# Weights' sign bits, the reciprocals' spread and a one-column minimum, from VectorE to GpSimd

## The chip, the core and the metric

The kernel runs on one core of a Trainium2 chip. The metric is the device time of one execution in microseconds (us). Engines are named as in the profile: PE (TensorE), DVE (VectorE), ACT (ScalarE), POOL (GpSimd) and SP (SyncE, which here only issues DMAs); PEld is PE's loading of weights.

## What is computed

Attention with a block-causal mask over 8 batches of 8 heads (576 tokens, head size 64), and on its output a two-layer feed-forward net with an unusual gate (`moe` in the names), 4608 tokens of width 512, hidden width 2048.

```
scores = scale * np.matmul(q, k.transpose(0, 1, 3, 2))
mask = block_i >= block_j
scores = np.where(mask, scores, -1000000000.0)
scores = scores - np.max(scores, axis=-1, keepdims=True)
attn = np.exp(scores)
attn = attn / (np.sum(attn, axis=-1, keepdims=True) + 1e-09)
attn_out = np.matmul(attn, v)
...
h = x @ w_in
sp = np.maximum(h, 0.0) + np.log1p(np.exp(-np.abs(h)))
g = h * erf(sp)
return (g @ w_out).astype(np.float32)
```

The weights come as 64-bit floats and are turned into numbers of the chip by the kernel itself.

## The kernel before

**Order.** Nothing runs in the order in which it is written. Every piece of work is recorded as a task by `Plan.add` (engine, assumed duration in ns, what it reads and writes, a priority), and `Plan.order` then plays the machine through with these assumed durations, always giving a free engine its ready task of the smallest priority. What comes out is one fixed instruction order for each engine; on the chip each engine works through its own list, and waits where an input or a buffer isn't there. Two things of this planner matter here. A DVE task that touches no PSUM is assumed to take longer while POOL is at work, by the share `SHARE` of what POOL's task still has to go. And the priority is a time in units of one head: head n has priority n, the decoding of the weights is spread from 0.5 and 6.5 on (`DEC0`, `DECR`), the net's units start at 12.5 (`MOE`) and follow each other by 0.93 (`STEP`).

**Weights** (`decode`, L326 to L331). Each of the 32 weight tiles arrives as 128 rows of 512 64-bit words (`raw`, four buffers in two tags). ACT scales the upper half of each word, read as a 32-bit float (L327). Two DVE instructions make a 32-bit word `sign` out of 16-bit quarters of the words: three low bits by a shift right by 13, and the sign bit by an and with 0x8000 (L329). A third DVE instruction shifts the scaled value left by 3 and ors `sign` in (L331). When all 16 tiles of a layer are there, their size is measured (L347 and what follows), and then each tile is split into two 16-bit parts, by ACT (L338) and DVE (L339).

**Heads** (64, in order). `split_qk` (L579, L580) splits keys and queries, and DMAs lay the parts out in one of three buffers `qk` (L583). `maxes` computes all scores `s` once on PE (L591); DVE takes the largest of every row, as six reductions (L595) of which the last two cover the halves of the fifth row block, and the minimum of these two (negated maxima, 64 rows by one column) is formed by L621. PE transposes the result (`mt`, L625), ACT copies it (L627) and a DMA puts it into `qk` as a further row, so that the second scores `t` (L643, L644) come with the maximum already taken off. ACT exponentiates (L648); the result is split in two parts `ph` and `pl`, of the first tile by ACT and DVE (L659, L661), of the second by POOL (L657, L661). PE multiplies with the values (`u`, L691) and sums (`us`, L720). `normalise` (four heads at a time) turns the sums by PE (`rt`, L738), takes reciprocals on DVE (L741), spreads them over columns into `rw` (L748, two instructions, DVE), transposes them on PE (`rb`, L755) and multiplies (L759, L762).

**The net** works in 72 units of 256 tokens by 512 hidden columns: PE `m_h` (L432), the gate on ACT and DVE (L392 to L414), PE `o` (L447).

**Filling.** 730 matmuls without a result (`warm`, L836) stand in PE's list between those of the first fourteen heads, by priority.

The values that `decode` takes with the shift and the and are whole 16-bit numbers; `words().bitcast(U16)` with t=4 names the quarters of a 64-bit word, quarter 3 holding the sign.

Of the kernel before, what the change touches and what calls it, by code (L numbers as in the profile page):

```python
# [13 lines left out]
U16 = mybir.dt.uint16  # L14
F32R = mybir.dt.float32r
AF = mybir.ActivationFunctionType
ALU = mybir.AluOpType
# [45 lines left out]
class Plan:  # L63
# [4 lines left out]
    SPARE = 300.0  # L68
    SWITCH = 90.0
    DRAIN = -0.7  # L70
    SHARE = 0.7
    HEAVY = 75.0
    ASIDE = 1.5

# [143 lines left out]
def tile_attention_moe(ctx: ExitStack, tc: tile.TileContext, qk, v, w, maskrows, sels, out):  # L218
    nc = tc.nc
    B, H, D2, S = qk.shape  # L220
    D = D2 // 2
    NT, DM = out.shape
    NF = w.shape[0]
    P = 128
# [18 lines left out]
    add = plan.add  # L243
# [71 lines left out]
    def decode(s, f):  # L315

        i = place(s, f)
        raw = buf("m", [P, UW], F32, ("r0", "r1")[f % 2], f"raw{s}_{f}", NR)
        words = lambda: raw()[:, : 2 * DM].bitcast(I32)
        top = lambda: words().rearrange("p (n t) -> p n t", t=2)[:, :, 1]  # L320
        val = lambda: home(i + 1)
        bits = lambda: val().bitcast(I32)
        bs = buf("m", [P, UW], F16, ("gh", "gl")[f % 2], f"sign{s}_{f}", NG)
        sign = lambda: bs().bitcast(I32)
        k, ks = ("W", i + 1), bs
        add("SP", 500, lambda: nc.sync.dma_start(words(), w[f, s].bitcast(I32)), w=[raw], lag=6000.0)  # L326
        add("ACT", 670, lambda: nc.scalar.activation(val(), f32(top()), AF.Copy, scale=2.0**-112), r=[raw], w=[k])  # L327
        for z, (op, val16) in enumerate(((ALU.logical_shift_right, 13), (ALU.bitwise_and, 0x8000))):
            add("DVE", 420, lambda z=z, op=op, val16=val16: nc.vector.tensor_scalar(out=sign().bitcast(U16).rearrange("p (n t) -> p n t", t=2)[:, :, z],  # L329
                in0=words().bitcast(U16).rearrange("p (n t) -> p n t", t=4)[:, :, 1 + 2 * z], scalar1=val16, scalar2=None, op0=op), r=[raw], w=[ks])  # L330
        add("DVE", 700, lambda: nc.vector.scalar_tensor_tensor(out=bits(), in0=bits(), scalar=3, in1=sign(), op0=ALU.logical_shift_left, op1=ALU.bitwise_or), r=[ks], w=[k])  # L331

    def split_weight(s, f):
# [251 lines left out]
    def maxes(n):  # L585
# [32 lines left out]
            red(4 + j, s, 0, 288, 64)  # L618

        def e():  # L620
            add("DVE", 300, lambda: nc.vector.tensor_tensor(out=mx[:64, 4:5], in0=mx[:64, 4:5], in1=mx[:64, 5:6], op=ALU.min), r=[("mx", n % 2, 5)], w=[("mx", n % 2, 4)])  # L621

        def f():
            pt = bank(f"mt{n}")
# [7 lines left out]
    def probs(n, out):  # L632

        K = D + 5
        sc = qsc[n // 4]
        klh, qhl, kh, qh = wide(n, 0), part(n, 1), wide(n, 2), part(n, 3)

        def one(j, q0, w_):
            kk = min(P, S - j * P)
            ks = slice(j * P, j * P + P)  # L640
            s = bank(f"t{j}_{n}_{q0}")

            add("PE", mmns(w_, True), lambda: nc.tensor.matmul(s()[:, :w_], lhsT=klh[:, ks], rhs=qhl[:, q0 : q0 + w_], start=True, stop=False), r=Q(n, "kl", "kc", "ql", "qc", "m"), w=[s])  # L643
            add("PE", mmns(w_, True), lambda: nc.tensor.matmul(s()[:, :w_], lhsT=kh[:K, ks], rhs=qh[:K, q0 : q0 + w_], start=False, stop=True), r=Q(n, "kh", "qh", "m"), w=[s])  # L644
            skip = max(0, starts[j] - q0)
            pt, c = offs[j]
            c += q0 + skip - starts[j]
            add("ACT", 190 + 0.84 * (w_ - skip), lambda: nc.scalar.activation(p32s[pt][n % NP[pt]][:kk, c : c + w_ - skip], s()[:kk, skip:w_], AF.Exp, scale=sc()[:kk, 1:2]),  # L648
                r=[s, sc], w=[("p32", pt, n % NP[pt], j, q0)])

        def split(pt, keys):
            p = p32s[pt][n % NP[pt]]
            ph = buf("a", [P, PN[pt]], F16, f"ph{pt}", f"ph{pt}_{n}", NPH)
            pl = buf("a", [P, PN[pt]], F16, f"pl{pt}", f"pl{pt}_{n}", NPH)
            keys = [("p32", pt, n % NP[pt], *k) for k in keys]
            if pt:
                add("POOL", 1100, lambda: nc.gpsimd.tensor_copy(ph(), p), r=keys, w=[ph])  # L657
            else:
                add("ACT", 850, lambda: nc.scalar.copy(ph(), p), r=keys, w=[ph])  # L659
            eng, ns, on = (("DVE", 1250, nc.vector), ("POOL", 2050, nc.gpsimd))[pt]  # L660
            add(eng, ns, lambda: on.tensor_tensor(out=pl(), in0=p, in1=ph(), op=ALU.subtract), r=keys + [ph], w=[pl])  # L661
            out.append((ph, pl))

        return [lambda: one(0, 0, 288), lambda: one(0, 288, 288), lambda: one(3, 320, 256),
                lambda: (one(4, 320, 256), split(0, [(0, 0), (0, 288), (3, 320), (4, 320)])), lambda: one(1, 128, 448),
                lambda: (one(2, 256, 320), split(1, [(1, 128), (2, 256)]))]

# [60 lines left out]
    def normalise(b, qd, usbs, rs, krs):  # L728
# [14 lines left out]
        def m(pp):  # L743
# [1 line left out]
            x16 = buf("a", [P, 2, S], F16, "x16", f"x16_{nm}_{pp}", 2)  # L745
            rw = buf("a", [P, 5, 2, D], F32, "rw", f"rw{nm}_{pp}", 1)
            for hf, k in enumerate((3, 2)):
                add("DVE", 430 - 100 * hf, lambda hf=hf, k=k: nc.vector.tensor_scalar(out=rw()[:, 3 * hf : 3 * hf + k], in0=ri()[:, pp, :k, hf, :].unsqueeze(3).broadcast_to([P, k, 2, D]),  # L748
                    scalar1=bsc[:, 8 * b + 2 + qd : 8 * b + 3 + qd], scalar2=None, op0=ALU.mult), r=[ri, ("bsc", b)], w=[(rw, hf)])
            for hf, (q0, q1) in enumerate(((0, 384), (384, 576))):  # L750
                rb = bank(f"rb{nm}_{pp}_{hf}")
# [194 lines left out]
```

## Time and profile before

| what | value |
|---|---|
| median of 3 runs | 1274.19 us (1273.89 to 1276.28) |
| the profiled execution, its own time | 1273.55 us |
| its span, first to last instruction | 1271.7 us |
| mean granted clock of PE | 0.974 |
| ACT busy | 935.4 us (74%) |
| DVE busy | 852.4 us (67%) |
| POOL busy | 177.2 us (14%), 154 instructions |
| read from and written to HBM | 55.61 MB and 18.87 MB |

The profile shows one execution. Its busy times are sums over instructions; a line of a group holds the source line, the engine, the operation, what is written and read, the shapes and the count, then busy us, the mean ns of one instruction, and the idle time of the engine just before them with what ended it. A line of the waits holds who waited for whom, the total in us, the number of times and the longest. A line of the timeline holds start and duration in us. PE's busy time is modelled: an instruction that is recorded as busy may stand in a pipeline.

### The profile page before, as it was taken

To read this page: it belongs to the slowest core of one execution; us is meant where nothing else is said; L and a number is where in the kernel's file an instruction comes from. 1 tells how busy PE (TensorE), PEld (TensorE's weight loads), DVE (VectorE), ACT (ScalarE), POOL (GpSimd) and SP (SyncE) were. 2 spreads that over 40 slices of the span, in tenths; PEclk is the share of its full clock that TensorE was granted. 3 is DMA by queue.
4 is the path that set the end of the run, shared out by engine and by line. 5 is a ranking of instruction groups with operands and counts; after the bars stand their busy time and mean duration, and the time that the engine had idled before them with its cause. 6 is when DMAs were issued, how large, how long until landed. Compare 5 with 4: busy or idle time off the path is not lost.

```text
span 1271.7 us, 25003 instructions
## 1 busy us (share of the span) xinstructions
PE 1199.7 (94%) x9984; PEld 834.3 (66%) x9984; DVE 852.4 (67%) x1689; ACT 935.4 (74%) x1517; POOL 177.2 (14%) x154
## 2 busy tenths in 40 slices
PE   5898899789999989999999999999999999999997
PEld 2577676456666667666676767666777677766664
DVE  5898799975757686867677676768677755433332
ACT  4687567777777777777677876877788877777774
POOL 0221212000111111112011111111101111000000
PEclk7899999889999999998999999999999999999999
DMA  7566551302313151323223231404122210010000
GB/s 242 164 196 203 159 150 45 99 15 72 98 41 101 41 143 41 85 67 100 75 76 87 67 101 41 126 16 136 48 84 62 74 56 20 27 49 28 18 18 17
DMA packets 80674, 104.52 MB, mean 82 GB/s; under 512 B 10399, under 2 KB 61599, under 8 KB 80558
## 3 DMA queue, kind: packets, MB, share of 16 engines
q1 hardware_dynamic: 69678, 93.39, 24.7%
q10 hardware_dynamic: 10880, 9.53, 3.2%
q8 instruction: 79, 1.29, 0.4%
q14 instruction: 37, 0.30, 0.1%
HBM read 55.61 MB, written 18.87 MB: 59 GB/s over the span
## 4 chain that ended last, share of the span: by engine, by line
PE 69%; ACT 6%; DVE 2%; issue 1%; DMA 1%; ACTq 1%; DVEq 0%
PE m_h L432 27%; PE o L447 26%; PE u L691 4%; ACT m_r L401 3%; PE s L591 3%; PE t L643 3%; PE t L644 2%; PE us L720 2%; ACT p L648 1%; PE rt L738 1%; PE rb L755 1%; DMA qk<-qhi 1%; DVE m_r L405 1%; ACTq L583 0%; DVE m_h L412 0%
## 5 line engine op out<-in xcount | busy, mean ns | idle before, releaser
L432 PE MATMUL m_h<-xh,wsb 128*128 128x256 f16 x2304 | 400.3, 274 | 4.3 <-ACT p L648 1.5
L432 PEld LDWEIGHTS <-wsb 128*128 128x128 f16 x3456 | 339.4, 98 | 57.8 <-issue 6.5
L401 ACT ACTIVATE m_r<-m_r,c 128x1024 f32<-128x1024 f32 x288 | 330.4, 1147 | 50.6 <-DVE m_r L405 32.4
L447 PE MATMUL o<-wsb,m_gh 128*128 128x512 f16 x1152 | 337.4, 384 | 12.2 <-ACT m_gh L413 12.2
L432 PE MATMUL m_h<-xl,wsb 128*128 128x256 f16 x1152 | 315.8, 274 | 0.0
L648 ACT ACTIVATE p<-t,qsc 128x288 f32<-128x288 f32 (+4 forms) x384 | 175.6, 479 | 107.8 <-PE t L644 104.0
L595 DVE TENSOR_REDUCE mx<-s 64x1 f32<-64x288 f32 (+4 forms) x384 | 166.3, 470 | 72.5 <-PE s L591 71.0
L447 PE MATMUL o<-wsb,m_gl 128*128 128x512 f16 x576 | 207.9, 382 | 0.0
L447 PEld LDWEIGHTS <-m_gh 128*128 128x128 f16 x1152 | 112.4, 98 | 128.5 <-ACT m_gh L413 15.2
L405 DVE SCALAR_TENSOR_TENSOR m_r<-m_r,m_r 128x1024 f32<-128x1024 f32 x72 | 90.3, 1254 | 157.3 <-ACT m_r L401 157.1
L657 POOL CAST ph<-p 128x768 f16<-128x768 f32 x64 | 63.5, 993 | 902.1 <-ACT p L648 838.3
L392 ACT ACTIVATE m_r<-m_h,c,bsc 128x512 f32<-128x512 f32 (+3 forms) x192 | 123.0, 671 | 36.1 <-PE m_h L432 35.7
L591 PE MATMUL s<-qk 68*128 68x256 f16 (+3 forms) x384 | 96.4, 314 | 28.9 <-DMA qk<-qhi 22.4
L643 PE MATMUL t<-qk 128*128 128x288 f16 (+3 forms) x384 | 114.5, 303 | 6.7 <-DVE mx L595 2.4
L412 DVE SCALAR_TENSOR_TENSOR m_h<-m_r,m_h 128x512 f32<-128x512 f32 x144 | 92.9, 689 | 40.8 <-ACT m_r L401 40.6
L644 PE MATMUL t<-qk 69*128 69x288 f16 (+3 forms) x384 | 114.5, 304 | 2.5 <-DMA qk<-mt 2.5
L836 PE MATMUL warm<-ident 128*128 128x256 f16 (+1 forms) x730 | 111.8, 289 | 1.5 <-POOL ident masks.py:199 1.5
L661 POOL TENSOR_TENSOR pl<-p,ph 128x768 f16<-128x768 f32 x64 | 111.2, 1737 | 5.1
L413 ACT CAST m_gh<-m_h 128x512 f16<-128x512 f32 x144 | 82.0, 585 | 31.9 <-DVE m_h L412 29.9
L414 DVE TENSOR_TENSOR m_gl<-m_h,m_gh 128x512 f16<-128x512 f32 x144 | 93.0, 682 | 10.6 <-ACT m_gh L413 9.4
L447 PEld LDWEIGHTS <-m_gl 128*128 128x128 f16 x576 | 56.6, 99 | 62.0 <-issue 1.3
L836 PEld LDWEIGHTS <-ident 128*128 128x128 f16 x730 | 71.8, 99 | 23.5 <-issue 2.5
(103 smaller groups left out, 1363.8 us busy)
## 6 DMA issues: line engine op xcount, KB each, us to landing
st<-qk SPq DMA_DIRECT2D x64, 288.0 KB
raw<-w SPq DMA_DIRECT2D x32, 512.0 KB
v<-v SPq DMA_DIRECT2D x16, 640.0 KB
qk<-qhi SPq DMA_DIRECT2D x128, 72.0 KB
qk<-qhi ACTq DMA_DIRECT2D x128, 72.0 KB
qk<-qlo SPq DMA_DIRECT2D x128, 72.0 KB
x_d<-x SPq DMA_DIRECT2D x32, 288.0 KB
out<-ob SPq DMA_DIRECT2D x36, 256.0 KB
```

Source lines behind the costliest of these rows:

```text
L392: add("ACT", 310 + 0.84 * w * (y - x) / T, lambda i=i, h=h, b=b, x=x, y=y, w=w: nc.scalar.activation(cut(br[0]()[:, i * w : (i + 1) * w], ...
L401: add("ACT", 300 + 0.834 * UW, lambda r=r, a=a, pp=pp: nc.scalar.activation(r(), a(), AF.Square, bias=const(pp[1]), scale=pp[0]), r=[a] + ...
L405: add("DVE", 160 + 1.05 * UW, lambda r=r, a=a, c=c, pp=pp, ops=ops: nc.vector.scalar_tensor_tensor(out=r(), in0=a(), scalar=pp[0], in1=c() ...
L432: nc.tensor.matmul(hk(k), lhsT=wf16(0, f, lo)[:, cc * P : (cc + 1) * P], rhs=x()[:, cc, :], start=cc == 0 and i == 0, stop=cc == NCC - 1 a ...
L447: nc.tensor.matmul(o[c](), lhsT=a()[:, sl], rhs=wf16(1, f, wlo), start=u == 0 and k == 0 and not lo and wlo == 0, stop=u == NU - 1 and k = ...
L591: add("PE", mmns(w_, True), lambda: nc.tensor.matmul(s()[:, c0 : c0 + w_], lhsT=qh[:K, i * P : i * P + P], rhs=kh[:K, k0 : k0 + w_], start ...
L595: add("DVE", 145 + 1.07 * w_, lambda: nc.vector.tensor_reduce(out=mx[:r, col : col + 1], in_=s()[:r, c0 : c0 + w_], axis=AX.X, op=ALU.max, ...
L643: add("PE", mmns(w_, True), lambda: nc.tensor.matmul(s()[:, :w_], lhsT=klh[:, ks], rhs=qhl[:, q0 : q0 + w_], start=True, stop=False), r=Q( ...
L644: add("PE", mmns(w_, True), lambda: nc.tensor.matmul(s()[:, :w_], lhsT=kh[:K, ks], rhs=qh[:K, q0 : q0 + w_], start=False, stop=True), r=Q( ...
L648: add("ACT", 190 + 0.84 * (w_ - skip), lambda: nc.scalar.activation(p32s[pt][n % NP[pt]][:kk, c : c + w_ - skip], s()[:kk, skip:w_], AF.Ex ...
L661: add(eng, ns, lambda: on.tensor_tensor(out=pl(), in0=p, in1=ph(), op=ALU.subtract), r=keys + [ph], w=[pl])
L836: t = add("PE", 220 if n is None else 150, lambda: nc.tensor.matmul(b_w()[:, : w * P], lhsT=ident16, rhs=ident16[:, None, :].broadcast_to( ...
```

## The change

`sign` is now made by two POOL instructions with arithmetic in place of bit operations: the low bits as value times 2^-13, at most 7; the sign bit as (value at least 32768) times 32768. The minimum L621 becomes a POOL instruction that takes the second column as a per-row scalar, and the spread L748 becomes a POOL instruction of the same form as before. The assumed durations of the tasks on POOL are new, as are two of the split's, and `SHARE` falls from 0.7 to 0.2.

```diff
-    SHARE = 0.7
+    SHARE = 0.2
...
-        for z, (op, val16) in enumerate(((ALU.logical_shift_right, 13), (ALU.bitwise_and, 0x8000))):
-            add("DVE", 420, lambda z=z, op=op, val16=val16: nc.vector.tensor_scalar(out=sign().bitcast(U16).rearrange("p (n t) -> p n t", t=2)[:, :, z],
-                in0=words().bitcast(U16).rearrange("p (n t) -> p n t", t=4)[:, :, 1 + 2 * z], scalar1=val16, scalar2=None, op0=op), r=[raw], w=[ks])
+        for z, (a, oa, b, ob) in enumerate(((2.0**-13, ALU.mult, 7.0, ALU.min), (32768.0, ALU.is_ge, 32768.0, ALU.mult))):
+            add("POOL", 700, lambda z=z, a=a, oa=oa, b=b, ob=ob: nc.gpsimd.tensor_scalar(out=sign().bitcast(U16).rearrange("p (n t) -> p n t", t=2)[:, :, z],
+                in0=words().bitcast(U16).rearrange("p (n t) -> p n t", t=4)[:, :, 1 + 2 * z], scalar1=a, scalar2=b, op0=oa, op1=ob), r=[raw], w=[ks])
...
-            add("DVE", 300, lambda: nc.vector.tensor_tensor(out=mx[:64, 4:5], in0=mx[:64, 4:5], in1=mx[:64, 5:6], op=ALU.min), r=[("mx", n % 2, 5)], w=[("mx", n % 2, 4)])
+            add("POOL", 150, lambda: nc.gpsimd.tensor_scalar(out=mx[:64, 4:5], in0=mx[:64, 4:5], scalar1=mx[:64, 5:6], scalar2=None, op0=ALU.min), r=[("mx", n % 2, 5)], w=[("mx", n % 2, 4)])
...
-                add("POOL", 1100, lambda: nc.gpsimd.tensor_copy(ph(), p), r=keys, w=[ph])
+                add("POOL", 1000, lambda: nc.gpsimd.tensor_copy(ph(), p), r=keys, w=[ph])
...
-            eng, ns, on = (("DVE", 1250, nc.vector), ("POOL", 2050, nc.gpsimd))[pt]
+            eng, ns, on = (("DVE", 1050, nc.vector), ("POOL", 1750, nc.gpsimd))[pt]
...
-                add("DVE", 430 - 100 * hf, lambda hf=hf, k=k: nc.vector.tensor_scalar(out=rw()[:, 3 * hf : 3 * hf + k], in0=ri()[:, pp, :k, hf, :].unsqueeze(3).broadcast_to([P, k, 2, D]),
+                add("POOL", 650 - 150 * hf, lambda hf=hf, k=k: nc.gpsimd.tensor_scalar(out=rw()[:, 3 * hf : 3 * hf + k], in0=ri()[:, pp, :k, hf, :].unsqueeze(3).broadcast_to([P, k, 2, D]),
                     scalar1=bsc[:, 8 * b + 2 + qd : 8 * b + 3 + qd], scalar2=None, op0=ALU.mult), r=[ri, ("bsc", b)], w=[(rw, hf)])
```

Since the planner's numbers change, it orders all engines anew. PE's list has the same instructions in another order.

DVE's list at its start before, from the scale of the first four heads to the first reductions (`sign_0` and `sign_1` are the words of the first two weight tiles, `qlo` a head's low part, `vm` and `vs` the values' scale):

```order
L329 TENSOR_SCALAR sign_0_225<-raw_0_167 128x512
L487 TENSOR_REDUCE vm_0_228<-v_0_0_163 128x1
L572 COPY qsc_235<-qb_230 128x2
L329 TENSOR_SCALAR sign_0_225<-raw_0_167 128x512
L331 SCALAR_TENSOR_TENSOR wsb<-wsb,sign_0_225 128x512
L492 TENSOR_REDUCE vs_0_247<-vt_0_240 1x1
L580 SCALAR_TENSOR_TENSOR qlo_252<-st_136,qsc_235,qhi_238 128x576
L580 SCALAR_TENSOR_TENSOR qlo_257<-st_142,qsc_235,qhi_249 128x576
L493 TENSOR_SCALAR vs_0_247<-vs_0_247 1x1
L494 RECIPROCAL vs_0_247<-vs_0_247 1x1
L329 TENSOR_SCALAR sign_1_263<-raw_1_172 128x512 x2
L331 SCALAR_TENSOR_TENSOR wsb<-wsb,sign_1_263 128x512
```

The same place of DVE's list in the changed kernel:

```order
L487 TENSOR_REDUCE vm_0_227<-v_0_0_163 128x1
L572 COPY qsc_240<-qb_231 128x2
L331 SCALAR_TENSOR_TENSOR wsb<-wsb,sign_0_223 128x512
L492 TENSOR_REDUCE vs_0_252<-vt_0_244 1x1
L493 TENSOR_SCALAR vs_0_252<-vs_0_252 1x1
L494 RECIPROCAL vs_0_252<-vs_0_252 1x1
L331 SCALAR_TENSOR_TENSOR wsb<-wsb,sign_1_235 128x512
L580 SCALAR_TENSOR_TENSOR qlo_270<-st_136,qsc_240,qhi_246 128x576
L503 COPY vsb_0_274<-vb_0_263 128x2
L580 SCALAR_TENSOR_TENSOR qlo_277<-st_142,qsc_240,qhi_259 128x576
L331 SCALAR_TENSOR_TENSOR wsb<-wsb,sign_2_248 128x512
```

The `sign` instructions are gone from DVE, three of the L331 stand ahead of the first reductions instead of two, and each of them now waits for POOL.

POOL's list before holds nothing but pairs of L657 and L661, two heads of which stand here (heads 2 and 3, `p_1_0` and `p_1_1` being the two buffers of the second probability tile):

```order
L657 CAST ph_2_778<-p_1_0_120 128x768
L661 TENSOR_TENSOR pl_2_794<-p_1_0_120,ph_2_778 128x768
L657 CAST ph_3_934<-p_1_1_121 128x768
L661 TENSOR_TENSOR pl_3_945<-p_1_1_121,ph_3_934 128x768
L657 CAST ph_4_1160<-p_1_0_120 128x768
```

POOL's list in the changed kernel around the same two heads, while the first layer's weights are decoded:

```order
L329 TENSOR_SCALAR sign_12_727<-raw_12_566 128x512 x2
L329 TENSOR_SCALAR sign_13_750<-raw_13_590 128x512 x2
L621 TENSOR_SCALAR mx_130<-mx_130 64x1
L329 TENSOR_SCALAR sign_14_841<-raw_14_759 128x512
L657 CAST ph_2_851<-p_1_0_120 128x768
L661 TENSOR_TENSOR pl_2_862<-p_1_0_120,ph_2_851 128x768
L329 TENSOR_SCALAR sign_14_841<-raw_14_759 128x512
L329 TENSOR_SCALAR sign_15_901<-raw_15_774 128x512 x2
L621 TENSOR_SCALAR mx_131<-mx_131 64x1
L657 CAST ph_3_966<-p_1_1_121 128x768
L661 TENSOR_TENSOR pl_3_980<-p_1_1_121,ph_3_966 128x768
L329 TENSOR_SCALAR sign_0_1155<-raw_0_1026 128x512 x2
```

The weights' `sign` words, each of which waits for the landing of its `raw`, now stand in one line with the heads' minima and with `ph`, which waits for ACT; all 16 tiles of the first layer stand ahead of head 3's `ph`, where DVE's list before had the L331 of ten tiles (`sign_0` to `sign_9`) ahead of head 3's L661.

## The prediction

> **What bounds the kernel now.** First the head of the page, with its 40 slices, each 31.8 us long.
>
> ```profile
> span 1271.7 us, 25003 instructions
> PE 1199.7 (94%) x9984; PEld 834.3 (66%) x9984; DVE 852.4 (67%) x1689; ACT 935.4 (74%) x1517; POOL 177.2 (14%) x154
> PE   5898899789999989999999999999999999999997
> DVE  5898799975757686867677676768677755433332
> PEclk7899999889999999998999999999999999999999
> ```
>
> PE is busy 94% of the span. From the tenth slice on it is at 9 nearly throughout, while DVE has fallen to 5 to 8; in slices two to eight DVE stands at 7 to 9, and there PE has holes. So there are two stages, and only the early one has DVE near its limit. The windows make this exact; their columns are busy us and count of PE, PEld, DVE, ACT and POOL, then granted clock, DMA share and GB/s.
>
> ```profile
> 0.00:13.00 13.00, 10.45 (x41) 4.28 (x41) 1.02 (x7) 5.91 (x14) 2.47 (x26) 1.00 0.76 268
> 13.00:190.00 177.00, 149.82 (x1446) 115.16 (x1447) 149.33 (x335) 117.30 (x239) 35.04 (x25) 0.92 0.60 180
> 190.00:284.00 94.00, 78.18 (x619) 53.05 (x617) 79.11 (x156) 69.93 (x111) 12.92 (x10) 0.89 0.20 55
> 284.00:1256.00 972.00, 952.94 (x7851) 658.68 (x7852) 619.10 (x1190) 738.17 (x1151) 126.73 (x94) 0.99 0.23 65
> 1256.00:1272.00 16.00, 8.33 (x30) 3.09 (x28) 3.81 (x5) 4.06 (x6) 0.00 (x0) 0.86 0.09 33
> ```
>
> From 13 to 190 us the weights are decoded, from 190 to 284 they are split while the net begins, and then heads and net run side by side. PE's list holds the same instructions after the change, so the time can fall only by PE's idle time and by what the clock takes. Idle are 27.2 us in the first window (177 - 149.8), 15.8 in the second, 19.1 in the 972 us of the third, 7.4 at the end. The clock takes 0.11 of 94 us, 10.3 us, in the second. In the first it takes 0.08 of 177, 14 us, but nearly all of that lies at the start, where PE runs filler. **What can be won lies before 284 us: 43.0 us of idle time and some 10 of clock.** Whose wait is it? The waits between 13 and 284 us:
>
> ```profile
> ACT p L648 <- PE t L644: 30.3, 29, 5.0
> PE s L591 <- DMA qk<-qhi: 18.8, 10, 6.0
> ACT wsb L338 <- DVE wsb L339: 14.2, 13, 3.4
> DVE mx L595 <- PE s L591: 13.9, 19, 2.8
> PE mt L625 <- DVE mx L621: 3.8, 1, 3.8
> PE o L447 <- ACT m_gh L413: 3.7, 1, 3.7
> ```
>
> 18.8 of the 43.0 us end with a DMA that brings a head's keys and queries, and 3.8 with the first head's minimum, in the startup. The rest, 20.4 us, is made of small waits on DVE and ACT. ACT waits 14.2 us for DVE's split, so behind the net's first units DVE is what comes last.
>
> **What is removed from DVE.** Groups of DVE up to 284 us:
>
> ```profile
> L329 DVE TENSOR_SCALAR sign<-raw 128x512 uint16<-128x512 uint16 x64 | 29.6, 501 | 0.0
> L339 DVE SCALAR_TENSOR_TENSOR wsb<-wsb,wrow 128x512 f16<-128x512 f32 x31 | 25.6, 825 | 2.1 <-ACT wsb L338 1.9
> L331 DVE SCALAR_TENSOR_TENSOR wsb<-wsb,sign 128x512 int32<-128x512 int32 x32 | 24.1, 753 | 0.9
> L661 DVE TENSOR_TENSOR pl<-p,ph 128x832 f16<-128x832 f32 x17 | 19.9, 1173 | 3.3 <-ACT ph L659 3.3
> L580 DVE SCALAR_TENSOR_TENSOR qlo<-st,qsc,qhi 128x576 f16<-128x576 f32 x20 | 17.6, 879 | 4.1 <-ACT qhi L579 4.1
> L621 DVE TENSOR_TENSOR mx<-mx 64x1 f32<-64x1 f32 x19 | 6.1, 322 | 0.1
> L748 DVE TENSOR_SCALAR rw<-ri,bsc 128x384 f32<-128x384 f32 x7 | 4.2, 597 | 0.0
> ```
>
> L329 gives 29.6 us, L621 6.1, and L748 4.2 with seven of its shorter form, 7 x 0.375 = 2.6 by its mean below. That is **42.5 us of DVE's 228.4 busy us between 13 and 284** (149.3 + 79.1), 19%. The three groups over the whole span stand below: after 284 us go 12 us of L621 and 25 x (0.602 + 0.375) = 24 us of L748 from a DVE that is busy 64% there; PE's 19.1 us of idle time in 972 is all that they could touch, and I count them as nothing. They are hidden behind PE's own list.
>
> ```profile
> L748 DVE TENSOR_SCALAR rw<-ri,bsc 128x384 f32<-128x384 f32 x32 | 19.3, 602 | 0.3
> L621 DVE TENSOR_TENSOR mx<-mx 64x1 f32<-64x1 f32 x64 | 18.0, 282 | 0.5
> L748 DVE TENSOR_SCALAR rw<-ri,bsc 128x256 f32<-128x256 f32 x32 | 12.0, 375 | 0.0
> ```
>
> **What POOL takes on.** Its groups up to 284 us:
>
> ```profile
> L661 POOL TENSOR_TENSOR pl<-p,ph 128x768 f16<-128x768 f32 x17 | 30.8, 1813 | 1.4
> L657 POOL CAST ph<-p 128x768 f16<-128x768 f32 x17 | 17.1, 1008 | 212.5 <-ACT p L648 193.4 <-PE s L591 11.1 <-PE t L643 7.9
> L472 POOL MEMSET rs<- 64x192 f32 x3 | 0.6, 253 | 0.0
> ```
>
> The trace shows no POOL instruction like the new ones. The nearest row is the cast: one input, one output. Over 512 in place of 768 columns it gives 1008 x 512/768 = 672 ns. From below the memset's 253 ns, with no input and fewer columns, bounds it; from above the two-input row, 1813 ns undivided. I take 0.67 us: 64 x 0.67 = 43 us for `sign`. L748 comes to 0.50 and 0.34 us in the same way, 6 us up to 284; L621, a single column, lies between nothing and the memset, 0.2 us or so, some 4 us for 19. POOL thus goes from 48 to about 101 us of 271: far from full. By the bounds `sign` would be 16 to 116 us, and POOL 74 to 174 of 271.
>
> The Trainium skill, page GPSIMD Engine Reference, section 3.1 (Elementwise), speaks against such a move: it keeps elementwise work on DVE, and gives 769 ns for a tight loop over 512 elements. By that figure, an estimate, `sign` would be 49 us; no run here shows it, and the sum would hardly differ.
>
> **What DVE loses again.** The two engines hold each other up. Rows of the timeline:
>
> ```profile
> 65.26 0.68 DVE L331 SCALAR_TENSOR_TENSOR wsb<-wsb,sign 128x512 int32<-128x512 int32 x1
> 72.14 1.13 POOL L657 CAST ph<-p 128x768 f16<-128x768 f32 x1 [7.29 <-ACT p L648]
> 72.48 0.79 DVE L621 TENSOR_TENSOR mx<-mx 64x1 f32<-64x1 f32 x1
> 83.99 0.97 POOL L657 CAST ph<-p 128x768 f16<-128x768 f32 x1 [8.87 <-ACT p L648]
> 84.31 1.19 DVE L331 SCALAR_TENSOR_TENSOR wsb<-wsb,sign 128x512 int32<-128x512 int32 x1
> ```
>
> An L331 with POOL idle takes 0.68 us. One that begins at 84.31, inside a cast that ends at 84.96, ends at 85.50: it stood still until POOL was done. The one-column minimum at 72.48 ended with the cast, at 73.27. Over the whole run the medians tell what such instructions take undisturbed (min/median/max):
>
> ```profile
> L331 DVE SCALAR_TENSOR_TENSOR wsb<-wsb,sign x32: 672/691/1312, 15.4 to 189.5; 128x512 int32<-128x512 int32 x32
> L339 DVE SCALAR_TENSOR_TENSOR wsb<-wsb,wrow x32: 719/747/2130, 181.7 to 284.1; 128x512 f16<-128x512 f32 x32
> L661 DVE TENSOR_TENSOR pl<-p,ph x64: 992/1012/2378, 39.5 to 1075.7; 128x832 f16<-128x832 f32 x64
> L580 DVE SCALAR_TENSOR_TENSOR qlo<-st,qsc,qhi x64: 797/810/2190, 18.1 to 1023.1; 128x576 f16<-128x576 f32 x64
> ```
>
> Against the means above, the loss up to 284 us is 32 x 62 ns = 2.0 us for L331, 31 x 78 = 2.4 for L339, 17 x 161 = 2.7 for L661 and 20 x 69 = 1.4 for L580: 8.5 us for 48 us of POOL, 0.18 per us. The 53 us that POOL takes on cost 9.5 at this rate. On top, an L331 comes when POOL has just finished its `sign` and may begin the next one: half an instruction each, 32 x 0.34 = 11 us at most; I take a third, 3.5. So DVE loses 13 and is **relieved by 42.5 - 13 = 29.5 us net**.
>
> **What becomes of it.** At most 20.4 us of idle time and 10.3 of clock, 31 in all, are within reach; the 18.8 us on the DMA are not, since keys and queries go through three buffers and their transfer as before. I take half of the idle time, 10, and a third of the clock, 3.5: the relief is 13% of DVE's early work, but the filler in PE's list is fixed in number and takes its time with DVE faster too. Against it stand new waits. The minimum now stands in POOL's list behind `sign` words that wait for their landing and behind `ph`, which waits for ACT; behind it wait `mt` on PE, and all that follows there. The cover is wide in the later stage:
>
> ```profile
> 342.43 0.14 DVE L621 TENSOR_TENSOR mx<-mx 64x1 f32<-64x1 f32 x1
> 346.04 0.27 PE L625 MATMUL mt<-ident,mx 128*5 128x128 f32 x1
> ```
>
> There PE takes the result 3.5 us after it is there, more than a cast and a two-input instruction of POOL (1.01 + 1.81 = 2.82 us). Without cover one head costs what the startup's wait cost, 3.8 us; I take one such, 4. The sum: 1273.55 - 10 - 3.5 + 4 = 1264.05, say **1264.5 us**, against the profiled execution's own 1273.55 (span 1271.7 and 1.85 around it); that execution lies 0.64 under the median of 1274.19.
>
> **Rivals.** *All of the relief arrives* (0.12): the new order closes the small waits and the clock stays up in the second window; 20.4 + 10.3 less 4 is 27, hence 1247. For it speaks that ACT waits for DVE there; against it that other engines are 74 to 83% busy too.
>
> *It was hidden anyway* (0.22): PE's early time is its filler, its DMA waits and the first units' chain through ACT (3.7 us on `m_gh`), and the relief only lets DVE wait longer, as it does already for 13.9 us on `s`. Then 1273.5, give or take 2.5. The other form of this is that the new instructions do not spare DVE anything, since the time that L621 spends waiting for POOL (mean 322 ns, 0.14 us in the row at 342.43) is spent on POOL's list instead.
>
> *POOL gives back more than it takes* (0.18), the one on the slow side. Place: L331 between 13 and 190 us. If a `sign` instruction takes as long as the two-input row, 1.81 us, POOL works 126 us more, which cost 0.18 x 126 = 23 us, and every L331 meets half an instruction, 32 x 0.9 = 29: 52 us lost against 42.5 won, DVE up by 9.5, time 1283. It decides from about 1.5 us per instruction on (0.18 x 106 + 32 x 0.75 = 43). Between the two the time lies between 1273.5 and 1283. The Trainium skill, page SBUF — State Buffer, section Who interferes with whom, tells of a pair of ports that VectorE and GpSimd share; whichever comes first holds it for its whole instruction, against a DVE instruction with two SBUF inputs too. By that rule every new POOL instruction can stop an L331; the row at 84.31 agrees.
>
> **How the numbers follow.** My forecast (1259 to 1270) has 0.48, the rivals 0.12, 0.22 and 0.18. A measurement of this kernel can tell some 0.2%, 2.5 us, from no change. Faster: 0.48 + 0.12 and a little of the second, 0.62. Same: 0.20. Slower: 0.18. For 8 in 10 the range leaves out the far half of the first rival and the far part of the last: 1250 to 1278.
>
> **What would show it.** Right: L329 on POOL near 0.67 us; DVE's busy time up to the last L339 down by about 30 us, and that L339 before 276 us in place of 284; L331's mean rising to 0.8 or 0.9 us; PE's idle time before the same place down by about 10; the later stage as it is. Wrong: `sign` at 1.5 us or more; L331 above 1.5; PE waiting for L621 on POOL in many heads; PE's waits for the DMA of `qhi` growing as the rest shrinks; or idle time coming up after 284 us, where all orders were made anew and I have assumed that PE does not mind.

## The result, and the profile after

The change makes the kernel slower: 1336.92 us (median of 4 runs, 1331.49 to 1338.15) against 1275.15 us (median of 4) for the kernel before on the same chip, a ratio of 1.0476 with a 95% interval of 1.0445 to 1.0508. The prediction said 1264.5. One execution of a later kernel, minimum and spread alone, took 1552.58 us at a granted clock of 0.751 and is left out of its median and ratio. The head of the page of the changed kernel:

```profile
span 1334.8 us, 25085 instructions
PE 1224.1 (92%) x9984; PEld 842.8 (63%) x9984; DVE 794.2 (59%) x1497; ACT 934.1 (70%) x1517; POOL 438.1 (33%) x346
PE   4587668998999999999999899999999999999997
DVE  3454447588675667676756666667676654443332
POOL 6998995121222222222213332323132323010000
PEclk7688769898999999999999999999999999999999
```

A slice is 33.4 us long. In the first six DVE has fallen from 5 to 9 to 3 to 5, as was wanted, but PE has fallen with it and POOL stands at 6 to 9. From slice eleven on PE is at 9 nearly throughout, as before. To measure this, take a point that both kernels pass: the fifth unit of the net, whose first matmul stands in the timelines (start, us, what) at 275.66 us before and at 336.31 after:

```profile
275.66 0.27 PE L432 MATMUL m_h<-xh,wsb 128*128 128x256 f16 x1
```

```profile
336.31 0.28 PE L432 MATMUL m_h<-xh,wsb 128*128 128x256 f16 x1
```

Three windows, the first 205 us, then up to that point and from there on, with the columns that the prediction gives; before:

```profile
0.00:205.00 205.00, 173.73 (x1600) 130.41 (x1601) 163.69 (x368) 134.93 (x270) 42.22 (x54) 0.93 0.58 177
...
13.00:276.00 263.00, 222.27 (x2015) 163.54 (x2016) 224.88 (x484) 180.01 (x341) 47.96 (x34) 0.91 0.48 141
276.00:1272.00 996.00, 967.00 (x7931) 666.45 (x7928) 626.48 (x1200) 749.45 (x1164) 126.73 (x94) 0.99 0.23 64
```

and after:

```profile
0.00:205.00 205.00, 136.15 (x983) 90.64 (x984) 93.40 (x190) 98.73 (x202) 180.33 (x120) 0.76 0.49 149
...
13.00:336.00 323.00, 241.73 (x1975) 170.60 (x1977) 189.81 (x373) 177.89 (x337) 215.53 (x126) 0.82 0.39 113
336.00:1335.00 999.00, 970.98 (x7974) 667.63 (x7968) 604.20 (x1123) 750.42 (x1168) 220.12 (x194) 0.99 0.23 65
```

The last rows are 996 and 999 us long, so **the loss lies before the net's fifth unit**: 60 us of it, for much the same number of matmuls (2015 and 1975). PE's idle time there grew from 40.7 us (263 - 222.27) to 81.3 (323 - 241.73), and its busy time by 19.5, with a clock of 0.82 in place of 0.91. In the first 205 us PE gets through 983 matmuls where it did 1600, while POOL is busy for 180 of the 205 us. What keeps POOL busy stands in its groups up to 345 us:

```profile
L329 POOL TENSOR_SCALAR sign<-raw 128x512 uint16<-128x512 uint16 x64 | 148.9, 2328 | 15.5 <-DMA raw<-w 11.5
L661 POOL TENSOR_TENSOR pl<-p,ph 128x768 f16<-128x768 f32 x16 | 28.2, 1764 | 1.4
...
L657 POOL CAST ph<-p 128x768 f16<-128x768 f32 x16 | 13.1, 821 | 8.4 <-ACT p L648 8.2
L621 POOL TENSOR_SCALAR mx<-mx 64x1 f32<-64x1 f32 x18 | 10.3, 574 | 69.6 <-DVE mx L595 44.6 <-DVE wone L359 14.3 <-DVE wmx L349 10.2
```

A `sign` instruction takes 2.33 us, not the 0.67 of the prediction; 64 of them are 149 us. With the 35 us that the heads' pairs took between 13 and 190 us before, that is 184 us, for a decoding whose last L331 started at 189.5 us then. It can't end before POOL is through; here the last `sign` instruction starts at 205.1 us and the last L331 at 224.1. The spread's groups on POOL, and DVE's four two-input groups up to 345 us:

```profile
L748 POOL TENSOR_SCALAR rw<-ri,bsc 128x384 f32<-128x384 f32 x6 | 9.0, 1498 | 9.3 <-DVE ri L741 9.0 <-PE warm L836 0.4
L748 POOL TENSOR_SCALAR rw<-ri,bsc 128x256 f32<-128x256 f32 x6 | 7.2, 1198 | 0.0
```

```profile
L339 DVE SCALAR_TENSOR_TENSOR wsb<-wsb,wrow 128x512 f16<-128x512 f32 x31 | 25.2, 812 | 4.8 <-ACT wsb L338 4.5
L331 DVE SCALAR_TENSOR_TENSOR wsb<-wsb,sign 128x512 int32<-128x512 int32 x32 | 25.1, 800 | 39.0 <-POOL sign L329 38.4 <-ACT wsb L327 0.6
L661 DVE TENSOR_TENSOR pl<-p,ph 128x832 f16<-128x832 f32 x17 | 19.4, 1138 | 11.4 <-ACT ph L659 11.4
L580 DVE SCALAR_TENSOR_TENSOR qlo<-st,qsc,qhi 128x576 f16<-128x576 f32 x20 | 17.7, 890 | 5.1 <-ACT qhi L579 5.0
```

L331 has risen only from 753 to 800 ns; what it costs is the 38.4 us of DVE's waiting for `sign`. The waits between 13 and 205 us show where PE stands (who waited for whom, us, times, longest):

```profile
PE mt L625 <- POOL mx L621: 41.9, 7, 11.0
DVE wsb L331 <- POOL sign L329: 38.4, 14, 6.0
...
DVE mx L595 <- PE s L591: 25.1, 10, 7.6
```

PE waits 41.9 us in seven pieces for the one-column minimum. One of them in the timeline (start, us, what, idle time before it):

```profile
153.58 10.63 POOL L329 TENSOR_SCALAR sign<-raw 128x512 uint16<-128x512 uint16 x5
...
164.16 0.29 POOL L621 TENSOR_SCALAR mx<-mx 64x1 f32<-64x1 f32 x1
164.24 1.76 DVE L331 SCALAR_TENSOR_TENSOR wsb<-wsb,sign 128x512 int32<-128x512 int32 x2 [5.26 <-POOL sign L329]
...
164.50 0.37 PE L625 MATMUL mt<-ident,mx 128*5 128x128 f32 x1 [6.79 <-POOL mx L621]
```

A minimum of 0.29 us stands behind five `sign` instructions, and PE stands with it for 6.79 us. So far the trace allows three causes: the minimum's place in POOL's list, the order of all lists, which was laid out for instructions of 0.7 us, and POOL's capacity, that is, more work than it can do in the time. The experiments take them apart.

### The profile page after: what moved, and what is told of

Its sections match the earlier page's. It is cut to its first block, busy times and chain, and to the rows that moved or that the text cites. A ratio compares the mean times of both kernels' runs of the same rounds, so it can differ in the third digit from the quotient of the medians.

```text
span 1334.8 us, 25085 instructions
## 1 busy us (share of the span) xinstructions
PE 1224.1 (92%) x9984; PEld 842.8 (63%) x9984; DVE 794.2 (59%) x1497; ACT 934.1 (70%) x1517; POOL 438.1 (33%) x346
## 4 chain that ended last, share of the span: by engine, by line
PE 67%; POOL 14%; ACT 7%; DVE 5%; issue 3%; DMA 2%; ACTq 1%; SPq 0%; POOLq 0%
PE m_h L432 26%; PE o L447 24%; POOL sign L329 9%; PE u L691 4%; POOL rw L748 3%; PE s L591 3%; ACT m_r L401 3%; PE t L643 2%; PE t L644 2%; DMA qk<-qhi 2%; PE us L720 2%; ACT p L648 1%; DVE mx L595 1%; PE rt L738 1%; POOL pl L661 1%
## 5 line engine op out<-in xcount | busy, mean ns | idle before, releaser
L621 POOL TENSOR_SCALAR mx<-mx 64x1 f32<-64x1 f32 x64 | 43.5, 680 | 409.0 <-DVE mx L595 362.5
L329 POOL TENSOR_SCALAR sign<-raw 128x512 uint16<-128x512 uint16 x64 | 148.9, 2328 | 15.5 <-DMA raw<-w 11.5
L836 PE MATMUL warm<-ident 128*128 128x256 f16 (+1 forms) x730 | 131.9, 315 | 1.5 <-POOL ident masks.py:199 1.5
L748 POOL TENSOR_SCALAR rw<-ri,bsc 128x384 f32<-128x384 f32 x64 | 77.0, 1209 | 144.6 <-DVE ri L741 130.8
L591 PE MATMUL s<-qk 68*128 68x256 f16 (+3 forms) x384 | 100.2, 323 | 20.7 <-DMA qk<-qhi 12.0
L661 POOL TENSOR_TENSOR pl<-p,ph 128x768 f16<-128x768 f32 x64 | 111.6, 1743 | 5.5
L657 POOL CAST ph<-p 128x768 f16<-128x768 f32 x64 | 56.8, 887 | 159.6 <-ACT p L648 159.1
```

Of the source, the lines that this page charges most:

```text
L329: add("POOL", 700, lambda z=z, a=a, oa=oa, b=b, ob=ob: nc.gpsimd.tensor_scalar(out=sign().bitcast(U16).rearrange("p (n t) -> p n t", t=2)[ ...
L591: add("PE", mmns(w_, True), lambda: nc.tensor.matmul(s()[:, c0 : c0 + w_], lhsT=qh[:K, i * P : i * P + P], rhs=kh[:K, k0 : k0 + w_], start ...
L836: t = add("PE", 220 if n is None else 150, lambda: nc.tensor.matmul(b_w()[:, : w * P], lhsT=ident16, rhs=ident16[:, None, :].broadcast_to( ...
```

## The experiments

The ratios are to the kernel before on the same chip, with 95% intervals. "Told" is the duration that `Plan.add` is given, from which the orders of all engines come.

**One part alone, with the change's numbers.** Three kernels: `sign` alone on POOL, the minimum and the spread alone, and the numbers alone with all three parts on DVE. The edits against the changed kernel; for the first:

```diff
-            add("POOL", 150, lambda: nc.gpsimd.tensor_scalar(out=mx[:64, 4:5], in0=mx[:64, 4:5], scalar1=mx[:64, 5:6], scalar2=None, op0=ALU.min), r=[("mx", n % 2, 5)], w=[("mx", n % 2, 4)])
+            add("DVE", 300, lambda: nc.vector.tensor_tensor(out=mx[:64, 4:5], in0=mx[:64, 4:5], in1=mx[:64, 5:6], op=ALU.min), r=[("mx", n % 2, 5)], w=[("mx", n % 2, 4)])
...
-                add("POOL", 650 - 150 * hf, lambda hf=hf, k=k: nc.gpsimd.tensor_scalar(out=rw()[:, 3 * hf : 3 * hf + k], in0=ri()[:, pp, :k, hf, :].unsqueeze(3).broadcast_to([P, k, 2, D]),
+                add("DVE", 430 - 100 * hf, lambda hf=hf, k=k: nc.vector.tensor_scalar(out=rw()[:, 3 * hf : 3 * hf + k], in0=ri()[:, pp, :k, hf, :].unsqueeze(3).broadcast_to([P, k, 2, D]),
```

> Only the sign words are made on POOL; the minimum and the spread are back on DVE; the planner's numbers are those of the change. Theory A (POOL's time: a sign instruction takes 2.1 to 2.3 us instead of 0.7, 64 of them fill POOL between 13 and 205 us, and whatever else stands in its list, minima above all, comes late): the minima no longer stand behind sign words, so PE's 42 us of waits on L621 go; but DVE still waits for sign at L331 and reductions behind it, so half or more of the loss stays: 1295 to 1320 us. Theory B (the planner's new numbers make worse orders by themselves): about as slow as the change, 1325 to 1340. Theory C (POOL holds up DVE's two-input instructions): as A, but with L331's mean well above the 0.80 us of the change.

For the second, L329 goes back instead (for the third, all of it):

```diff
-        for z, (a, oa, b, ob) in enumerate(((2.0**-13, ALU.mult, 7.0, ALU.min), (32768.0, ALU.is_ge, 32768.0, ALU.mult))):
-            add("POOL", 700, lambda z=z, a=a, oa=oa, b=b, ob=ob: nc.gpsimd.tensor_scalar(
...
+        for z, (op, val16) in enumerate(((ALU.logical_shift_right, 13), (ALU.bitwise_and, 0x8000))):
+            add("DVE", 420, lambda z=z, op=op, val16=val16: nc.vector.tensor_scalar(
...
```

> The sign words are back on DVE; minimum and spread on POOL, the planner's numbers of the change. Theory A: POOL is free again before 205 us, the kernel is within 10 us of the one before (1265 to 1285). Theory B: still 1310 or more, since the planner's numbers are the change's. A rival within A, the later stage: rw at 1.25 and 0.92 us on POOL in front of PE's transposes costs a few us there.

> All three pieces are on DVE as before; only the planner's numbers are those of the change (SHARE 0.2, and 1000, 1750 and 1050 ns for the split). Theory A: as before within 6 us (1268 to 1281). Theory B: most of the loss, 1310 or more.

Measured: `sign` alone 1337.6 us, 1.0502 (1.0456 to 1.0548); minimum and spread alone 1285.55 us (median of eight), 1.0077 (1.0053 to 1.01); the numbers alone 1278.12 us, 1.0025 (1.0004 to 1.0047). `sign` alone costs as much as the whole change. Its minimum is on DVE, so **the minimum's place isn't the cause**: the seven waits for L621 are where the delay shows. The first kernel landed where theory B was expected, yet the third refutes B: the new numbers by themselves cost a quarter of a per cent. The first kernel too tells the planner 700 ns for a `sign` instruction, which neither theory took into account. With the minimum gone from POOL, other waits stand there (the waits of that kernel between 13 and 345 us):

```profile
DVE wsb L331 <- POOL sign L329: 36.1, 13, 4.9
...
PE s L591 <- DMA qk<-qhi: 25.2, 12, 5.3
```

**The change with true durations told.** It keeps every instruction of the change, and alters only what the planner believes (2330 is the mean in the trace, the others are near the shortest durations there; lines that end in `tensor_scalar(` are cut short, in all edits shown):

```diff
-            add("POOL", 700, lambda z=z, a=a, oa=oa, b=b, ob=ob: nc.gpsimd.tensor_scalar(
+            add("POOL", 2330, lambda z=z, a=a, oa=oa, b=b, ob=ob: nc.gpsimd.tensor_scalar(
...
-            add("POOL", 150, lambda: nc.gpsimd.tensor_scalar(
+            add("POOL", 300, lambda: nc.gpsimd.tensor_scalar(
...
-                add("POOL", 650 - 150 * hf, lambda hf=hf, k=k: nc.gpsimd.tensor_scalar(
+                add("POOL", 1260 - 340 * hf, lambda hf=hf, k=k: nc.gpsimd.tensor_scalar(
```

> The change as it is, but the planner is told what the instructions took: 2330 ns for a sign word, 300 for the minimum, 1260 and 920 for the spread. Theory A in its form of a wrong plan (PE's list was laid out for 0.7 us): the planner puts minima ahead of sign words and fills PE, and most of the loss goes, 1275 to 1300. Theory A in its form of plain capacity (149 us of sign work on one engine before the net can start): little is won, 1310 to 1335, since decoding ends at 200 us or later in either order.

Measured: 1296.74 us, 1.0184 (1.0148 to 1.0219). Of the 4.8%, **2.9 are the order** (1.0476 - 1.0184) **and 1.8 remain**. Its window of the first 205 us, its splits L339 (duration min/median/max in ns, first and last start), and PE's waits for the minimum between 13 and 324 us:

```profile
0.00:205.00 205.00, 165.87 (x1410) 118.58 (x1411) 129.49 (x267) 111.29 (x228) 176.31 (x126) 0.91 0.57 176
```

```profile
L339 DVE SCALAR_TENSOR_TENSOR wsb<-wsb,wrow x32: 732/750/2130, 143.5 to 324.0; 128x512 f16<-128x512 f32 x32
```

```profile
PE mt L625 <- POOL mx L621: 5.4, 5, 2.8
```

POOL is busy for nearly as long as in the change (176 and 180 us of 205), but PE gets through 1410 matmuls in place of 983, at a clock of 0.91 in place of 0.76, and its waits for L621 have fallen from 41.9 us to 5.4: the heads are held behind `sign` words far less. What the new order doesn't do is end the weights' work early: the last split starts at 324.0 us, 284.1 before.

The same for `sign` alone, the minimum and the spread on DVE: the edit of the first kernel above, with

```diff
-            add("POOL", 700, lambda z=z, a=a, oa=oa, b=b, ob=ob: nc.gpsimd.tensor_scalar(
+            add("POOL", 2330, lambda z=z, a=a, oa=oa, b=b, ob=ob: nc.gpsimd.tensor_scalar(
```

> Sign words alone on POOL, the planner told 2330 ns. Against e1_sign_only (+5.0%, told 700) it shows what the wrong plan cost, against e4_true_costs (+1.8%) what minimum and spread add behind the sign words. Plan wrong by 3.3 times as the main cause: 1285 to 1300. If minima on POOL matter beside the sign words even in a right plan, it is well below e4: 1278 to 1286.

Measured: 1299.7 us, 1.0187 (1.0154 to 1.022). It is the same split, 3.15% order and 1.9% left over, without the other two parts. So both are `sign`'s. POOL's time between 13 and 200 us points at capacity for what is left over, 172.8 of 187 us:

```profile
13.00:200.00 187.00, 152.79 (x1377) 115.76 (x1378) 128.56 (x277) 109.74 (x223) 172.83 (x85) 0.89 0.57 174
```

**What does such an instruction cost, and why?** A kernel in which the weight tiles are decoded in turn by six forms of the POOL instruction (it doesn't make the `sign` words, so its time says nothing):

```diff
+        quarter = lambda z: words().bitcast(U16).rearrange("p (n t) -> p n t", t=4)[:, :, 1 + 2 * z]
+        half = lambda z: sign().bitcast(U16).rearrange("p (n t) -> p n t", t=2)[:, :, z]
+        def two(z):
+            nc.gpsimd.tensor_scalar(out=half(z), in0=quarter(z), scalar1=2.0**-13, scalar2=7.0, op0=ALU.mult, op1=ALU.min)
+        def one(z):
+            nc.gpsimd.tensor_scalar(out=half(z), in0=quarter(z), scalar1=2.0**-13, scalar2=None, op0=ALU.mult)
+        def copied(z):
+            nc.gpsimd.tensor_copy(half(z), quarter(z))
+        def dense(z):
+            nc.gpsimd.tensor_scalar(out=sign().bitcast(U16)[:, DM * z : DM * z + DM], in0=words().bitcast(U16)[:, DM * z : DM * z + DM], scalar1=2.0**-13, scalar2=7.0, op0=ALU.mult, op1=ALU.min)
+        def floats(z):
+            nc.gpsimd.tensor_scalar(out=sign().bitcast(F32), in0=f32(top()), scalar1=0.5, scalar2=1.0, op0=ALU.mult, op1=ALU.min)
+        def floats1(z):
+            nc.gpsimd.tensor_scalar(out=sign().bitcast(F32), in0=f32(top()), scalar1=0.5, scalar2=None, op0=ALU.mult)
+        form = (two, one, copied, dense, floats, floats1)[f % 6]
+        for z in range(2):
+            add("POOL", 700, lambda z=z: form(z), r=[raw], w=[ks])
```

> A measurement, its time means nothing: the 32 weight tiles take turns in six forms of the POOL instruction, all over 512 elements (all but the first leave out the sign words' making): two operations on 16-bit numbers as in the change; one operation; a copy; two operations on 16-bit numbers that lie densely; two operations on 32-bit floats; one operation on 32-bit floats. If the second operation makes it 2.1 us, one operation takes about 1.2; if the 16-bit conversion does, the float form takes about 1.2; if the strided access does, the dense form does; the copy should take 0.55 to 0.7.

The instructions on `sign`, in the order of the code (duration min/median/max in ns, first and last start):

```profile
L332 POOL TENSOR_SCALAR sign<-raw x12: 2087/2228/3182, 13.3 to 154.4; 128x512 uint16<-128x512 uint16 x12
L335 POOL TENSOR_SCALAR sign<-raw x12: 1648/1688/2537, 17.7 to 167.2; 128x512 uint16<-128x512 uint16 x12
L338 POOL COPY sign<-raw x12: 753/770/1566, 21.6 to 161.8; 128x512 uint16<-128x512 uint16 x12
L341 POOL TENSOR_SCALAR sign<-raw x12: 1918/1920/2258, 24.2 to 175.6; 128x512 uint16<-128x512 uint16 x12
L344 POOL TENSOR_SCALAR sign<-raw x8: 1943/1959/3022, 28.5 to 143.2; 128x512 f32<-128x512 f32 x8
L347 POOL TENSOR_SCALAR sign<-raw x8: 1505/1518/1992, 33.5 to 158.5; 128x512 f32<-128x512 f32 x8
```

By the minima a copy takes 0.75 us. The same elements with one multiplication take 1.65, more than twice that; a second operation adds 0.44, and the strides 0.17 (2087 - 1918). The float forms read every second word, so type and stride aren't quite separated there; but at 1.94 and 1.51 they lie within 0.15 us of the 16-bit forms. It is the step from copy to arithmetic that costs most, not the 16-bit words.

**Would it have paid at the predicted duration?** The change with its own numbers, and copies in place of the two instructions, which leave the making of the `sign` words out:

```diff
+        for z in range(2):
+            add("POOL", 700, lambda z=z: nc.gpsimd.tensor_copy(sign().bitcast(U16).rearrange("p (n t) -> p n t", t=2)[:, :, z],
+                words().bitcast(U16).rearrange("p (n t) -> p n t", t=4)[:, :, 1 + 2 * z]), r=[raw], w=[ks])
```

> The change with its own plan, but the two sign instructions are plain copies of the same 512 quarters (this leaves out the making of the low bits and of the sign, so the weights are wrong). It gives the instruction roughly the duration that the prediction assumed. Theory A (all of the loss is the instruction's duration): the kernel comes to 1260 to 1290, the upper part if the minimum and the spread cost what they cost without the sign words on POOL (+0.8%). Theory D (it is POOL's list as such, the wait for landings in front of minima and ph, whatever the duration): 1310 or more.

Measured: 1279.7 us, 1.005 (1.0015 to 1.0086). The copies took 0.76 us in the median and 0.90 in the mean, somewhat above the 0.67 of the prediction. In the traces this kernel and the change run the same list of lines and tiles on PE, on DVE and on POOL. So **4.3 of the 4.8% (1.0476 - 1.005) hang on the duration of these 64 instructions alone**: the order fits 0.7 us well enough and 2.33 badly. And still nothing is won. To see whether the numbers of the other two parts are in the way, minimum and spread alone were run with true ones, `sign` being on DVE:

```diff
-            add("POOL", 150, lambda: nc.gpsimd.tensor_scalar(
+            add("POOL", 300, lambda: nc.gpsimd.tensor_scalar(
...
-                add("POOL", 650 - 150 * hf, lambda hf=hf, k=k: nc.gpsimd.tensor_scalar(
+                add("POOL", 1260 - 340 * hf, lambda hf=hf, k=k: nc.gpsimd.tensor_scalar(
```

> Minimum and spread on POOL, sign words on DVE, and the planner told 300 ns for the minimum and 1260 and 920 for the spread (it was 150, 650 and 500). If the +0.8% of the same kernel with the planner's wrong numbers is a matter of the plan: 1270 to 1280. If it is the longer way itself (1.25 + 0.92 us in front of PE's transposes, one more engine between reductions and PE): 1282 to 1292.

Measured: 1270.15 us, 0.9951 (0.9925 to 0.9978), half a per cent faster than the kernel before. The same two parts with the change's numbers were at 1.0077, so 1.3% hangs on these three numbers of the planner. Whether any other order would have done as well isn't shown; but of three pairs so far that differ in such numbers alone, the one with the truer numbers is faster each time, and the next is a fourth. The copies once more, with these numbers and 900 told for themselves:

> As e6_copy (copies in place of the making of the sign words, which leaves them out; mean 0.90 us there), and the planner told 900, 300 and 1260 and 920 ns. All the instructions of the change's kind are off DVE, POOL is cheap, the plan is right: this is the state that the prediction meant. If DVE's relief of 42 us before 284 us is worth the 9 us that were forecast beyond what minimum and spread give: 1255 to 1264. If the relief is worth nothing, since PE's early time is its own: 1266 to 1275, as e9_no_sign_true.

Measured: 1266.81 us, 0.9936 (0.991 to 0.9961). Its window up to 276 us, and PE's two longest groups of waits in it:

```profile
13.00:276.00 263.00, 222.75 (x2019) 163.71 (x2020) 197.09 (x373) 181.06 (x343) 134.71 (x128) 0.92 0.48 141
```

```profile
PE s L591 <- DMA qk<-qhi: 15.7, 10, 4.6
...
PE mt L625 <- POOL mx L621: 4.1, 2, 3.1
```

Against the same window before, DVE is relieved by 27.8 us (224.88 - 197.09), nearly the 29.5 of the prediction, and PE has the same busy time, the same count and 40.2 us of idle time in place of 40.7. **The relief is real and worth nothing there.** The decoding ends earlier (the last L331 starts at 156.9 us, 189.5 before), and PE still waits for the keys and queries. This also tells what the 1.8% left over aren't. They aren't the longer way through a second engine, which the copies take as well, nor DVE's instructions held up by POOL's: reckoned as in the prediction, its four groups lose some 13 us with the copies and 16 in the change with true durations, for 30 us between the two times. What differs, besides the order, is how long POOL is busy.

One rival no run tests. The filler is the larger part of PE's early work; its rows in the first 205 us, before and in the change:

```profile
L836 PE MATMUL warm<-ident 128*128 128x256 f16 x648 | 97.2, 275 | 0.0
L836 PE MATMUL warm<-ident 128*128 128x512 f16 x80 | 24.4, 402 | 1.5 <-POOL ident masks.py:199 1.5
```

```profile
L836 PE MATMUL warm<-ident 128*128 128x256 f16 x369 | 69.1, 309 | 0.0
L836 PE MATMUL warm<-ident 128*128 128x512 f16 x80 | 27.3, 439 | 1.5 <-POOL ident masks.py:199 1.5
```

Before, 121.6 of PE's 173.73 busy us are filler, and its count is fixed. Whether DVE's relief would be worth something with less of it stays open.

**Half of `sign`.** Low bits on POOL (2330 told), sign bit, minimum and spread on DVE:

```diff
+        add("POOL", 2330, lambda: nc.gpsimd.tensor_scalar(out=half(0), in0=quarter(0), scalar1=2.0**-13, scalar2=7.0, op0=ALU.mult, op1=ALU.min), r=[raw], w=[ks])
+        add("DVE", 420, lambda: nc.vector.tensor_scalar(out=half(1), in0=quarter(1), scalar1=0x8000, scalar2=None, op0=ALU.bitwise_and), r=[raw], w=[ks])
```

> Only the low bits are made on POOL (2330 ns for the planner), the sign bit, the minimum and the spread stay on DVE. 75 us of POOL instead of 149. Capacity (POOL's time bounds the decoding): decoding ends near 190 us again and the kernel is within 1% of before, 1265 to 1288. Theory D: POOL's in-order list still holds back ph and DVE's L331, 1295 or more.

Measured: 1282.2 us, 1.005 (1.0025 to 1.0076). POOL's group there:

```profile
L330 POOL TENSOR_SCALAR sign<-raw 128x512 uint16<-128x512 uint16 x32 | 72.1, 2253 | 20.5 <-DMA raw<-w 16.4 <-DVE pl L662 1.5 <-DVE rw L749 0.6
```

These 72 us lie between the 43 that the prediction gave to all of `sign` and the 149 that it took. The time is 0.5% above before; the change's other numbers, which this kernel and the next two also have, gave 0.25% alone, and the intervals overlap. With half of the work most of the loss is gone, and nothing is won either.

**Spread alone and minimum alone**, each with its true duration told, the rest on DVE (the edits as above, one part each):

> The spread alone on POOL (planner told 1260 and 920), minimum and sign words on DVE. e9_no_sign_true, with the minimum too, was at -0.5%. If the gain is the spread's (31 us of DVE's time): 1266 to 1272. If the minimum's: 1273 to 1279.

> The minimum alone on POOL (planner told 300), spread and sign words on DVE. If the gain of e9_no_sign_true is the minimum's (18 us of DVE's time, of which half was waiting for POOL): 1266 to 1272. If the spread's: 1273 to 1279.

Measured: spread 1268.55 us (median of 10, 1263.4 to 1273.88), 0.9948 (0.9926 to 0.997); minimum 1275.26 us, 1.0012 (0.9989 to 1.0034). So the half per cent of the two together is there with the spread alone, and moving only the minimum makes no difference that can be measured. **The spread alone on POOL, with its duration told rightly, is half a per cent faster than the kernel before.**

## Why the prediction was wrong, point by point

**The frame held.** PE's instructions are the same, and the loss lies before the net's fifth unit; the later stage took 999 us after 996, though POOL did 93 us more there. That 24 + 12 us less of DVE's work are worth nothing in it was nearly right: the spread's gain of half a per cent is what it missed. Where it lies the runs don't show: the profiled execution of the spread alone, at 1273.88 us, doesn't have the gain; in that of minimum and spread the fifth unit begins some 8 us earlier than before and the rest takes no less, while in that of the copies it begins 3 us earlier and the rest takes 7 us less. Taking the spread off DVE and the new order can't be separated either.

**What POOL takes on was the first step to fail.** "The nearest row is the cast": 0.67 us per `sign` instruction were 2.33, outside the upper bound of 1.81 too: an instruction with two operations on one input took longer than one with two inputs on more columns (1.76). The spread was put at 0.50 and 0.34 us and took 1.50 and 1.20 up to 345 us; the minimum was put at 0.2 and took 0.57. A cast is a copy; the form measurement shows that a copy's price can't be scaled to arithmetic. "Far from full" fell with it: POOL was busy for 180 of the first 205 us. The Trainium skill, page GPSIMD Engine Reference, section 3.1, gives 769 ns for 512 elements of a tight loop; the copy agrees with that at 753 to 770, but `tensor_scalar` does not, at 1.5 to 2.2 us, and the measurement decides.

**The order was the second, and was no step at all.** The account of the change noted that the `sign` words of 16 tiles now stand ahead of head 3's `ph`; the prediction counted one new wait of 4 us for it and took for granted that the order would fit. It was computed with 700 ns for 2330. The change with true numbers shows that this is the larger part, 2.9 of 4.8%. The rest, 1.8%, goes with the duration as well, since it is gone with the copies. That it is capacity is a reading: 149 us of `sign` and 35 of the heads' pairs all but fill the 189.5 us that the decoding took, with no room for waits.

**L331's duration came out, the rate behind it didn't.** Foretold were 0.8 to 0.9 us beside `sign` instructions of 0.67. With the copies, which come near to that, L331 had 0.82 in the mean; that it had 0.80 beside instructions of 2.33 us is luck. Reckoned as in the prediction (the medians are within 4 ns of those before), the four groups lose 32 x 108 ns, 31 x 69, 17 x 127 and 20 x 82: 9.4 us, against 8.5 before, for some 217 us of POOL. That is 0.04 us per us of POOL and not 0.18: a rate some four times too high and a duration more than three times too low cancelled. Why the rate is lower the runs don't show. The slow rival had the right sign, but the wrong place; its point of 1.5 us no run tests. The loss was not DVE instructions held by POOL instructions, 52 us in all, but DVE and PE waiting for POOL's list, 38.4 and 41.9 us. Its 1283 had no term for that. "PE waiting for L621 on POOL in many heads" was named as a sign of failure and came, seven times; `sign` alone shows that it is a symptom.

**What becomes of the relief was the third.** "Half of the idle time and a third of the clock" were 13.5 us. With copies of 0.76 us DVE was relieved as foretold and PE's idle time stayed at 40.2 us; against the minimum and the spread without any relief from `sign` (0.9951), the copies with both (0.9936) win 0.15%, which the intervals can't tell from nothing. That this kernel comes near to 1264.5 is luck as far as `sign` goes: the spread alone gives as much. So for `sign` the rival "hidden anyway" was the right one at the predicted duration. That DVE was busy for 84% of the time between 13 and 284 us was no evidence that DVE's time sets PE's: the largest wait of PE there ended with a DMA.

## What to carry to other kernels

Before work goes to another engine, look for a row of the same operation on that engine; a copy says little about arithmetic, and with no such row the range has to be wide upwards, and whether the receiving engine fills up there decides the sign. Where a planner or a hand-made order uses assumed durations, run the change once more with the measured ones before judging it: here three fifths of the loss were the order, and for the two small parts the numbers alone turned 0.8% slower into 0.5% faster. An engine that is 84% busy is a candidate, not a bound: ask which wait of the bounding engine ends with it.

## What the runs showed of the hardware

POOL's `tensor_scalar` over 512 elements per row took 1.5 to 1.65 us with one operation and 1.9 to 2.1 with two, with at most 0.17 us between the strided, dense and float forms of the same number of operations, where POOL copied the same in 0.75 us, and DVE took 0.50 us in the mean for each of the `sign` instructions that were moved. Where PE stood idle more, its matmuls also ran more slowly: over the first 205 us the granted clock was 0.76 in the change and 0.93 before, and the same filler matmul took 309 ns in place of 275 in the mean. Together with the idle time that made 617 matmuls of difference, 279 of them filler.
